# Where GpSimd's operand sums stand among its other work, in a retention and feed-forward kernel on one core

## The chip, the core and the metric

The kernel runs on one NeuronCore of a Trainium2 chip. TensorE (PE in the profile) does the matmuls, with weight loads shown apart as PEld; VectorE (DVE), ScalarE (ACT) and GpSimd (POOL) do the elementwise work; SyncE (SP) issues nearly all DMAs, in program order on one queue. The metric is device time in microseconds (us) for the whole program, one launch.

## The reference

A retention layer (attention without softmax, with a fixed decay) feeds a two-layer feed-forward network with the activation h·cos(h):

```python
B, H, S, D_ = q.shape                       # 8, 8, 576, 64
scores = scale * np.matmul(q, k.transpose(0, 1, 3, 2))
gamma = 1.0 - 2.0 ** (-5.0 - np.arange(H))
Dmat = np.where(rel >= 0, gamma[:, None, None] ** rel[None, :, :], 0.0)   # rel = i - j
x = np.matmul(scores * Dmat, v)             # then reshaped to 4608 tokens x 512
h = x @ w_in                                # 512 -> 2048
g = h * np.cos(h)
out = g @ w_out                             # 2048 -> 512, float32
```

## The kernel before, in words

**Groups.** The 4608 tokens are 36 groups of 128. `load(g)` issues the DMAs for q, k and v of one group on SP's queue. `prep(g)` runs on GpSimd (lines 137, 138 and 144; line 146 once in nine groups): it scales q and k by their share of the decay, casts v, and leaves bf16 tiles `qks` and `vb`. `transposes(g)` (line 153) is from group 6 on a DMA on SP's queue that turns `qks` into `qkT`; for groups 4 and 5 TensorE does it. Retention is then matmuls per group: `scores` (line 180, masked by VectorE into `ret`, line 189), `states` (line 239, summed by VectorE, lines 260 and 262) and `attn_out` (lines 280 and 293, evacuated into `xT`, line 305).

**Tiles.** The feed-forward part walks ten tiles of tokens, n = 0 to 9, of widths 512, 256, 256 and then seven times 512. For a tile, `mm1` (line 320) computes h for 1024 columns at a time into PSUM; ScalarE takes the cosine (line 328) and VectorE multiplies (line 329) into `gT`, of which there is one buffer. Tiles 0 to 2 multiply with `w_out` plainly (`mm2`, line 337). Tiles 3 to 9 (from `S7 = 3` on) use `mm2_seven`: the product of a 2x2 block split is made from seven block products (line 430) in the order 3, 4, 5, 2, 1, 7, 6, instead of eight. Products 3 and 4 need differences of quarters of `w_out` (`w_sums(3)` and `w_sums(4)`, written in place into `w_out_sb`); products 1, 6 and 7 need three more sums of quarters (`ws`); products 5, 2, 1, 7 and 6 need sums of quarters of `gT` (`gs`, made by `g_sum`, line 395). `gs5` is made on VectorE, the others on GpSimd, except `gs1` of tile 3. From tile 4 on they are made in two halves, after the fourth and the eighth `mm1` block; in tile 3 the first part of `gs5` and `gs2` is emitted after the seventh block and all the rest after the eighth. Each product is 16 matmuls.

**What sets the order.** The scheduler is in manual mode: each engine runs its instructions in the order in which the program emits them. The retention work of coming groups is put between the products of a tile by hand, through `at` (`scores2` and `unit7`, ahead of the product named). `feed(s)` is called each time a block of 128 output tokens is stored (s = 0 to 35, four per wide tile), just after the store's DMA was emitted, and it emits the next `prep`, `transposes` and `load` calls. So on GpSimd the sums of a tile stand ahead of the preparation that `feed` emits during that tile's products, and on SP's queue stores, transposing DMAs and loads stand in the order of the calls. The tile pools hold 5 loaded groups (`ld`), 8 prepared (`nat`) and 8 transposed ones (`trp`); an instruction that writes a buffer waits for the last reader of what it held.

The rule by which `feed` decides, before (late tiles prepare only what had been loaded by an earlier call):

```python
while prepared < min(before if s >= late_from else loaded, NG, 2 * s + 7, s + 11):
    prep(prepared)
```

The functions that the diff touches, with the line numbers of the profile:

Of the kernel before, what the change touches and what calls it, by code (L numbers as in the profile page):

```python
# [13 lines left out]
ALU = mybir.AluOpType  # L14
# [3 lines left out]
def kernel(  # L18
# [16 lines left out]
    nc = tc.nc  # L35
# [18 lines left out]
    assert sum(widths) == NTOK  # L54
    starts = [sum(widths[:n]) for n in range(len(widths))]
    N_PE_T = 6

    consts = ctx.enter_context(tc.tile_pool(name="consts", bufs=1))
    first = ctx.enter_context(tc.tile_pool(name="first", bufs=1))
    ld = ctx.enter_context(tc.tile_pool(name="ld", bufs=5))  # L60
    nat = ctx.enter_context(tc.tile_pool(name="nat", bufs=8))
    trp = ctx.enter_context(tc.tile_pool(name="trp", bufs=8))
    retp = ctx.enter_context(tc.tile_pool(name="retp", bufs=4))
# [86 lines left out]
    def transposes(g, banks=None, only=(0, 1)):  # L150
        qks, vb, qkT, qT = tiles["a", g]
        if g >= N_PE_T:
            nc.sync.dma_start(qkT, qks.rearrange("s m h d -> s (m h d)"), transpose=True)  # L153
            return
        for m in only:
            ps = psum.tile([P, HG, P], BF16, tag=banks[m], name="tr")
            for hg in range(HG):
                nc.tensor.transpose(
                    ps[:, hg, :],
                    qks[:, m, 2 * hg : 2 * hg + 2, :].rearrange("s h d -> s (h d)"),  # L160
                    ident,
                )
            nc.scalar.copy(qkT[:, m * HG : (m + 1) * HG, :], ps)
        if ("fv", g) in tiles and g != 3:
            nc.scalar.copy(vb, tiles.pop(("fv", g)))
# [193 lines left out]
    def w_sums(x, e0, e1):  # L359

        a, b, op_ = {
            3: ((0, 1), (1, 1), ALU.subtract),
            4: ((1, 0), (0, 0), ALU.subtract),
            1: ((0, 0), (1, 1), ALU.add),
            6: ((0, 0), (0, 1), ALU.add),
            7: ((1, 0), (1, 1), ALU.add),
        }[x]
        if x in (3, 4):
            w_sum[x] = w_quarter(*a)
        elif x not in w_sum:  # L370
            pool, tag = {1: (consts, "ws1"), 6: (first, "qs4"), 7: (first, "qT4")}[x]
            w_sum[x] = pool.tile([P, E2, N2], BF16, tag=tag, name=f"ws{x}")
        nc.vector.tensor_tensor(
            out=w_sum[x][:, e0:e1],
            in0=w_quarter(*a)[:, e0:e1],
            in1=w_quarter(*b)[:, e0:e1],
            op=op_,
        )

    def g_sum(n, x, e0, e1):  # L380

        gT = tiles["g", n]
        a, b, op_ = {
            5: ((0, 0), (0, 1), ALU.add),
            2: ((1, 0), (1, 1), ALU.add),
            1: ((0, 0), (1, 1), ALU.add),
            7: ((0, 1), (1, 1), ALU.subtract),
            6: ((1, 0), (0, 0), ALU.subtract),
        }[x]
        if ("gs", n, x) not in tiles:  # L390
            tiles["gs", n, x] = sump.tile([P, E2, 256], BF16, tag=f"gs{x}", name=f"gs{x}")
        i0, i1 = (
            gT[:, k * E2 + e0 : k * E2 + e1, r * 256 : (r + 1) * 256] for r, k in (a, b)
        )
        (nc.vector if x == 5 or (n, x) == (S7, 1) else nc.gpsimd).tensor_tensor(  # L395
            out=tiles["gs", n, x][:, e0:e1], in0=i0, in1=i1, op=op_
        )

    def sums_after(n, i):

        if n == S7:
            if i < 4:
                w_sums(3 + i % 2, i // 2 * 4, i // 2 * 4 + 4)
            if i == 6:
                g_sum(n, 5, 0, 4)
                g_sum(n, 2, 0, 4)
            elif i == 7:
                for x, e in ((5, 4), (2, 4), (1, 0), (7, 0), (6, 0)):
                    g_sum(n, x, e, E2)
        elif i in (3, 7):  # L410
            for x in (5, 2, 1, 7, 6):
                g_sum(n, x, i - 3, i + 1)
# [26 lines left out]
    def mm2_seven(n, at):  # L439

        s0 = starts[n] // P

        def new(tag):
            return op.tile([P, 2, N2], F32, tag=tag, name="ot")

        def store(t, r, c, s):
            r0 = starts[n] + r * 256
            nc.sync.dma_start(
                out[r0 : r0 + 256, c * N2 : (c + 1) * N2].rearrange("(j p) c -> p j c", p=P), t
            )  # L450
            feed(s)

        for x in (3, 4, 5, 2, 1, 7, 6):
            for u in at.get(x, []):
                u()
            product(n, x)
            if x == 3:
                u22 = new("a")
                nc.scalar.copy(u22, tiles["o", 3])
            elif x == 4:  # L460
                nc.vector.tensor_tensor(out=u22, in0=tiles["o", 4], in1=u22, op=ALU.add)
            elif x == 5:
                c12, u11 = new("c"), new("b")
                nc.scalar.copy(c12, tiles["o", 3])
                nc.vector.tensor_tensor(out=u11, in0=u22, in1=tiles["o", 3], op=ALU.subtract)
                store(c12, 0, 1, s0)
            elif x == 2:
                c21 = new("d")
                nc.scalar.copy(c21, tiles["o", 4])
                nc.vector.tensor_tensor(out=u22, in0=u22, in1=tiles["o", 4], op=ALU.subtract)  # L470
                store(c21, 1, 0, s0 + 1)
            elif x == 1:
                nc.vector.tensor_tensor(out=u11, in0=tiles["o", 1], in1=u11, op=ALU.add)
            elif x == 7:
                nc.vector.tensor_tensor(out=u11, in0=tiles["o", 7], in1=u11, op=ALU.add)
                store(u11, 0, 0, s0 + 2)
            elif x == 6:
                nc.vector.tensor_tensor(out=u22, in0=tiles["o", 1], in1=u22, op=ALU.add)
                store(u22, 1, 1, s0 + 3)
# [3 lines left out]
    def feed(s):  # L483

        nonlocal loaded, prepared, transposed
        before = loaded
        late_from = starts[S7] // P
        while True:
            while prepared < min(before if s >= late_from else loaded, NG, 2 * s + 7, s + 11):
                prep(prepared)  # L490
                prepared += 1
                if transposed < N_PE_T:
                    transposed += 1

            if N_PE_T <= transposed < min(prepared, s + 11) and (
                transposed <= loaded - 2 or loaded == NG or (s > 3 and loaded == before)
            ):
                transposes(transposed)
                transposed += 1
            elif loaded < min(NG, 2 * s + 8, s + 13):  # L500
                load(loaded)
                loaded += 1
            else:
                break
# [131 lines left out]
        if not soon:  # L636
            copy()

    def unit7(g, more=True):

        copy = states([g + 1, g + 2], "b")()
        attn_out([g, g + 1], "m", nc.scalar.copy)
        if more:
            scores2(g + 2)
        copy(nc.scalar.copy)

    late = []
    for n, w in enumerate(widths):
# [14 lines left out]
        for i, (et, c0, cw) in enumerate(blocks):  # L663

            inside = {
                (0, 0): {2: lambda: (attn_out([3], "n"), state(3))},
                (1, 0): {4: lambda: scores(5, "a")},
                (1, 1): {3: lambda: attn_out([5], "a", evac=nc.scalar.copy)},
            }.get((n, i), {})
            mm1(n, et, c0, cw, banks[i], inside)  # L670
            if (n, i) == (3, 1):
                late.pop()()
            if n == 2 and i < 3:
                for e in (0, 4):
                    w_sums((1, 6, 7)[i], e, e + 4)
            if n >= S7:
                sums_after(n, i)

        g = starts[n] // P + w // P
        if n == 0:  # L680
            todo = [
                (45, lambda: transposes(4, "ab")),
                (49, lambda: state(4)),
                (50, lambda: scores(4, "a")),
                (57, lambda: attn_out([4], "a")),
                (61, lambda: transposes(5, "ba")),
                (63, lambda: state(5)),
            ]
        elif n == 1:
            todo = pair(6, "ab", 16, 27)  # L690
        elif n == 2:
            todo = [(11, lambda: scores2(g)), (25, lambda: unit(g, "m", soon=True))]
            late += [lambda: unit(g + 2, "b", False)]
        else:
            at = {}
            if n + 1 < len(widths):
                at = {5: [lambda: unit7(g)], 1: [lambda: unit7(g + 2, n > S7)]}
                if n in (3, 4):
                    at[4] = [lambda: scores2(g)]
            mm2_seven(n, at)  # L700
            continue
        todo.sort(key=lambda u: u[0])
# [42 lines left out]
```

## Time and profile before

| what | value |
|---|---|
| time, median of 6 runs | 324.21 us (323.46 to 325.91) |
| the profiled execution's own time | 323.46 us |
| its span on the core | 321.8 us, mean granted TensorE clock 0.991 |
| TensorE busy | 293.7 us (91%) |
| GpSimd busy | 218.5 us (68%) |
| VectorE busy | 210.1 us (65%) |
| ScalarE busy | 139.3 us (43%) |
| sums on GpSimd (line 395) | 52 instructions, 116.0 us |

All positions in the text are us from the start of the profiled span. The profiled execution spends 1.7 us outside the span (323.46 less 321.8). A busy share is a mean over stages with different limits, so the views used below are those with positions: the timelines of single engines, which give start, duration, engine, line, operation, tiles and, in square brackets, how long the engine had been idle just before and what ended that; the list of waits (total us, times, longest); and the chain of work that ended last.

### The profile page before, as it was taken

The numbers are of one execution on the slowest core, as the hardware profiler recorded it, in microseconds if no ns is written. First come the engines' busy times: TensorE is split into PE (matmuls) and PEld (weight loads), VectorE is DVE, ScalarE is ACT, GpSimd is POOL, SyncE is SP. The second block draws the span as 40 slices with busy tenths as digits, with TensorE's granted clock in tenths as the row PEclk, the third lists the DMA queues.
The fourth block names the chain that finished last, engine by engine and source line by source line (L and its number), as shares of the span: only waits on it lengthen the run. The fifth ranks groups of instructions, "written<-read, shape, count | busy, mean of one in ns | idle before, by whom it ended". The sixth has DMA issues, their size and how long they took to land.

```text
span 321.8 us, 6585 instructions
## 1 busy us (share of the span) xinstructions
PE 293.7 (91%) x2724; PEld 199.5 (62%) x2745; DVE 210.1 (65%) x242; ACT 139.3 (43%) x176; POOL 218.5 (68%) x179
## 2 busy tenths in 40 slices
PE   8899999996998697997999899989998899899984
PEld 3478458573487585456745674567557754784573
DVE  5776335659499972687658765776478548935762
ACT  3656225232155252642356334633464346425610
POOL 2760165455544799599967996799769946950893
PEclk9999999999799999999999999999999999999998
DMA  8999999999999994999199909990999060021012
GB/s 210 210 212 207 196 226 207 172 203 251 155 237 182 233 205 93 232 215 171 37 223 212 208 3 194 245 212 7 181 242 209 26 163 2 0 67 65 2 55 76
DMA packets 154109, 50.23 MB, mean 156 GB/s; under 512 B 140768, under 2 KB 153056, under 8 KB 154080
## 3 DMA queue, kind: packets, MB, share of 16 engines
q1 hardware_dynamic: 149856, 45.63, 73.7%
q0 software_dynamic: 4224, 4.19, 7.9%
q8 instruction: 21, 0.34, 0.4%
q14 instruction: 8, 0.07, 0.1%
HBM read 36.70 MB, written 9.44 MB: 143 GB/s over the span
## 4 chain that ended last, share of the span: by engine, by line
PE 38%; POOL 24%; DMA 16%; SPq 11%; DVE 4%; issue 4%; ACT 2%; POOLq 1%
PE h L320 20%; POOL gs L395 17%; PE o L430 8%; DMA fq<-in_q_dram 7%; SPq L112 7%; DMA fk<-in_k_dram 6%; PE o L337 6%; SPq L153 3%; POOL qks L138 3%; DMA fv<-in_v_dram 2%; POOL qks L137 2%; ACT cosh L328 2%; DVE gT L329 2%; POOL vb L144 2%; PE sc L180 1%
## 5 line engine op out<-in xcount | busy, mean ns | idle before, releaser
L395 POOL TENSOR_TENSOR gs<-gT 128x1024 bf16<-128x1024 bf16 (+1 forms) x52 | 116.0, 2266 | 20.4 <-DVE gT L329 20.4
L320 PE MATMUL h<-xT,w_in_sb 128*128 128x512 bf16 (+2 forms) x820 | 127.2, 313 | 1.7 <-DVE gT L329 0.9
L329 DVE TENSOR_TENSOR gT<-h,cosh 128x1024 bf16<-128x1024 f32 x72 | 87.9, 1222 | 42.6 <-ACT cosh L328 42.6
L328 ACT ACTIVATE cosh<-h,half_pi 128x1024 f32<-128x1024 f32 x72 | 80.2, 1113 | 81.0 <-PE h L320 77.6
L320 PEld LDWEIGHTS <-w_in_sb 128*128 128x128 bf16 x832 | 76.0, 98 | 50.1 <-issue 1.7
L137 POOL TENSOR_TENSOR qks<-fq,gq 128x512 bf16<-128x512 f32 x32 | 34.7, 1084 | 60.0 <-DMA fq<-in_q_dram 57.9
L430 PEld LDWEIGHTS <-gs 128*128 128x128 bf16 x560 | 53.0, 98 | 17.1 <-POOL gs L395 9.0
L138 POOL TENSOR_TENSOR qks<-fk,gk 128x512 bf16<-128x512 f32 x35 | 36.9, 1054 | 13.6 <-DMA fk<-in_k_dram 13.0
L189 DVE TENSOR_TENSOR ret<-sc,tri 128x1024 bf16<-128x1024 f32 x32 | 37.9, 1216 | 4.8 <-PE sc L180 4.7
L430 PE MATMUL o<-ws,gs 128*128 128x256 bf16 x336 | 38.6, 273 | 2.1 <-POOL gs L395 2.1
L337 PE MATMUL o<-w_out_sb,gT 128*128 128x512 bf16 x121 | 30.3, 393 | 2.7 <-DVE gT L329 2.3
L430 PE MATMUL o<-w_out_sb,gs 128*128 128x256 bf16 x224 | 26.5, 273 | 5.3 <-POOL gs L395 4.6
L305 ACT CAST xT<-ov 128x1024 bf16<-128x1024 f32 (+1 forms) x18 | 16.5, 917 | 31.3 <-PE ov L293 31.2
L430 PE MATMUL o<-w_out_sb,gT 128*128 128x256 bf16 x224 | 25.9, 273 | 0.0
L430 PEld LDWEIGHTS <-gT 128*128 128x128 bf16 x224 | 21.7, 98 | 4.0
L144 POOL CAST vb<-fv 128x512 bf16<-128x512 f32 x32 | 20.9, 652 | 3.1 <-DMA fv<-in_v_dram 2.6
L337 PEld LDWEIGHTS <-gT 128*128 128x128 bf16 x128 | 12.1, 100 | 16.4 <-issue 2.7
L395 DVE TENSOR_TENSOR gs<-gT 128x1024 bf16<-128x1024 bf16 (+1 forms) x15 | 17.4, 1168 | 0.4
L180 PE MATMUL sc<-qkT 64*128 64x128 bf16 x256 | 12.2, 220 | 5.9 <-DVE s L262 3.7
L253 ACT CAST sb<-s 64x256 bf16<-64x256 f32 x40 | 16.1, 403 | 0.6
L180 PEld LDWEIGHTS <-qkT 64*128 64x128 bf16 x288 | 8.6, 95 | 12.3 <-issue 8.2
L347 ACT COPY ot<-o 128x512 f32<-128x512 f32 x8 | 4.7, 588 | 22.1 <-PE o L337 22.1
(72 smaller groups left out, 181.7 us busy)
## 6 DMA issues: line engine op xcount, KB each, us to landing
out_dram<-ot SPq DMA_DIRECT2D x36, 256.0 KB, 3.9
fk<-in_k_dram SPq DMA_DIRECT2D x32, 256.0 KB, 5.0
fv<-in_v_dram SPq DMA_DIRECT2D x32, 256.0 KB, 5.1
fq<-in_q_dram SPq DMA_DIRECT2D x28, 256.0 KB, 4.1
w_in_sb<-in_moe_w_in_dram POOLq DMA_DIRECT2D x4, 512.0 KB, 9.0
w_out_sb<-in_moe_w_out_dram POOLq DMA_DIRECT2D x4, 512.0 KB, 16.2
fq<-in_q_dram SPq DMA_DIRECT2D x2, 512.0 KB, 4.4
fq<-in_q_dram SPq DMA_DIRECT2D x8, 128.0 KB, 4.4
```

The costliest lines, as they stand in the source:

```text
L112: i = nc.sync.dma_start(f[p0:p1], src[b, :, s0 : s0 + p1 - p0, :].rearrange("h s d -> s h d"))
L137: nc.gpsimd.tensor_tensor(out=qks[:, 0], in0=fq, in1=tq, op=ALU.mult)
L138: (nc.vector if g == 3 else nc.gpsimd).tensor_tensor(out=qks[:, 1], in0=fk, in1=tk, op=ALU.mult)
L144: nc.gpsimd.tensor_copy(vb, fv)
L180: nc.tensor.matmul(ps[:, he, hg, :], lhsT=qkT[d0 : d0 + D, HG + hg, :], rhs=qT[d0 : d0 + D, hg, :], start=True, stop=True,)
L189: nc.vector.tensor_tensor(out=ret.rearrange("p a b i -> p (a b) i"), in0=ps.rearrange("p a b i -> p (a b) i"), in1=mask.unsqueeze(1).to_br ...
L320: nc.tensor.matmul(ps[:, j, :], lhsT=w_in_sb[:, dg, (et + j) * P : (et + j + 1) * P], rhs=xT[:, dg, c0 : c0 + w], start=(dg == 0), stop=(d ...
L328: nc.scalar.activation(cosh, ps, ACTF.Sin, bias=half_pi, scale=1.0)
L329: nc.vector.tensor_mul(gT[:, et : et + m, c0 : c0 + w], ps, cosh)
L337: nc.tensor.matmul(ps, lhsT=gT[:, et, tsi * P : (tsi + 1) * P], rhs=w_out_sb[:, et, :], start=(et == 0), stop=(et == ET - 1),)
L395: (nc.vector if x == 5 or (n, x) == (S7, 1) else nc.gpsimd).tensor_tensor(out=tiles["gs", n, x][:, e0:e1], in0=i0, in1=i1, op=op_)
L430: nc.tensor.matmul(ps[:, j], lhsT=lhs[:, e, j * P : (j + 1) * P], rhs=rhs[:, e, :], start=(x in (3, 4, 1, 7) and e == j == 0), stop=(e == ...
```

## The change

Six edits, all in the order or the place of work; what is computed stays the same.

1. `w_sums(3)` and `w_sums(4)` run on GpSimd, each as one instruction over 128x2048, emitted after the first `mm1` block of tile 3. Before, they were four VectorE instructions over 128x1024 after the first four blocks.
2. `w_sums` for 1, 6 and 7 (six VectorE instructions) move from tile 2's `mm1` into the `mm2` of tile 0.
3. In each half of a tile's `g_sum` calls the first sum on GpSimd gets a dependency on VectorE's `gs5` of the same half.
4. In tiles 3 and 4 the two `unit7` calls move from ahead of products 5 and 1 to ahead of products 2 and 7; in the others VectorE's addition `both` is emitted after the `states` additions of the first unit, not before them.
5. From s = 8 on (tile 3 and later) `feed` prepares to a count per store, 0, 1, 1 and 2 groups, and the transposing DMAs follow at once.
6. From s = 8 on `feed` then loads until five groups are loaded ahead of those prepared. For s below 8 its rule is as before.

Built, the program has on SP's queue the same order of DMAs as before up to the first store of tile 3, and on GpSimd the same order but for the two `w_out_sb` sums, which stand behind the preparation of group 17 and ahead of tile 3's `gs`.

```diff
@@ -54,10 +54,11 @@
     assert sum(widths) == NTOK
     starts = [sum(widths[:n]) for n in range(len(widths))]
     N_PE_T = 6
+    LD = 5
 
     consts = ctx.enter_context(tc.tile_pool(name="consts", bufs=1))
     first = ctx.enter_context(tc.tile_pool(name="first", bufs=1))
-    ld = ctx.enter_context(tc.tile_pool(name="ld", bufs=5))
+    ld = ctx.enter_context(tc.tile_pool(name="ld", bufs=LD))
     nat = ctx.enter_context(tc.tile_pool(name="nat", bufs=8))
     trp = ctx.enter_context(tc.tile_pool(name="trp", bufs=8))
     retp = ctx.enter_context(tc.tile_pool(name="retp", bufs=4))
@@ -370,7 +371,7 @@
         elif x not in w_sum:
             pool, tag = {1: (consts, "ws1"), 6: (first, "qs4"), 7: (first, "qT4")}[x]
             w_sum[x] = pool.tile([P, E2, N2], BF16, tag=tag, name=f"ws{x}")
-        nc.vector.tensor_tensor(
+        (nc.gpsimd if x in (3, 4) else nc.vector).tensor_tensor(
             out=w_sum[x][:, e0:e1],
             in0=w_quarter(*a)[:, e0:e1],
             in1=w_quarter(*b)[:, e0:e1],
@@ -392,15 +393,25 @@
         i0, i1 = (
             gT[:, k * E2 + e0 : k * E2 + e1, r * 256 : (r + 1) * 256] for r, k in (a, b)
         )
-        (nc.vector if x == 5 or (n, x) == (S7, 1) else nc.gpsimd).tensor_tensor(
+        i = (nc.vector if x == 5 or (n, x) == (S7, 1) else nc.gpsimd).tensor_tensor(
             out=tiles["gs", n, x][:, e0:e1], in0=i0, in1=i1, op=op_
         )
+        if x == 5:
+            tiles["gate"] = i
+        elif "gate" in tiles:
+            tc.add_manual_dep(
+                i.ins,
+                tiles.pop("gate").ins.name,
+                mybir.DependencyInfo(mybir.DependencyClass.Sync, mybir.DependencyReason.DATA),
+                reason="port free",
+            )
 
     def sums_after(n, i):
 
         if n == S7:
-            if i < 4:
-                w_sums(3 + i % 2, i // 2 * 4, i // 2 * 4 + 4)
+            if i == 0:
+                w_sums(3, 0, E2)
+                w_sums(4, 0, E2)
             if i == 6:
                 g_sum(n, 5, 0, 4)
                 g_sum(n, 2, 0, 4)
@@ -450,15 +461,18 @@
             )
             feed(s)
 
+        def both():
+            nc.vector.tensor_tensor(out=u22, in0=tiles["o", 4], in1=u22, op=ALU.add)
+
         for x in (3, 4, 5, 2, 1, 7, 6):
-            for u in at.get(x, []):
-                u()
+            if x in at:
+                at[x](*[both] * (x == 5))
+            elif x == 5:
+                both()
             product(n, x)
             if x == 3:
                 u22 = new("a")
                 nc.scalar.copy(u22, tiles["o", 3])
-            elif x == 4:
-                nc.vector.tensor_tensor(out=u22, in0=tiles["o", 4], in1=u22, op=ALU.add)
             elif x == 5:
                 c12, u11 = new("c"), new("b")
                 nc.scalar.copy(c12, tiles["o", 3])
@@ -484,9 +498,20 @@
 
         nonlocal loaded, prepared, transposed
         before = loaded
-        late_from = starts[S7] // P
+        n, r = divmod(s - starts[S7] // P, 4)
+        if n >= 0:
+            while prepared < min(NG, starts[S7] // P + 10 + 4 * n + (0, 1, 2, 4)[r]):
+                prep(prepared)
+                prepared += 1
+            while transposed < prepared:
+                transposes(transposed)
+                transposed += 1
+            while loaded < min(NG, prepared + LD):
+                load(loaded)
+                loaded += 1
+            return
         while True:
-            while prepared < min(before if s >= late_from else loaded, NG, 2 * s + 7, s + 11):
+            while prepared < min(loaded, NG, 2 * s + 7, s + 11):
                 prep(prepared)
                 prepared += 1
                 if transposed < N_PE_T:
@@ -636,9 +661,10 @@
         if not soon:
             copy()
 
-    def unit7(g, more=True):
+    def unit7(g, more=True, then=lambda: None):
 
         copy = states([g + 1, g + 2], "b")()
+        then()
         attn_out([g, g + 1], "m", nc.scalar.copy)
         if more:
             scores2(g + 2)
@@ -670,15 +696,15 @@
             mm1(n, et, c0, cw, banks[i], inside)
             if (n, i) == (3, 1):
                 late.pop()()
-            if n == 2 and i < 3:
-                for e in (0, 4):
-                    w_sums((1, 6, 7)[i], e, e + 4)
             if n >= S7:
                 sums_after(n, i)
 
         g = starts[n] // P + w // P
         if n == 0:
             todo = [
+                (34 + 5 * i, lambda x=x, e=e: w_sums(x, e, e + 4))
+                for i, (x, e) in enumerate((x, e) for x in (1, 6, 7) for e in (0, 4))
+            ] + [
                 (45, lambda: transposes(4, "ab")),
                 (49, lambda: state(4)),
                 (50, lambda: scores(4, "a")),
@@ -694,9 +720,16 @@
         else:
             at = {}
             if n + 1 < len(widths):
-                at = {5: [lambda: unit7(g)], 1: [lambda: unit7(g + 2, n > S7)]}
+                at = {
+                    5: lambda then: unit7(g, True, then),
+                    1: lambda: unit7(g + 2),
+                }
                 if n in (3, 4):
-                    at[4] = [lambda: scores2(g)]
+                    at = {
+                        4: lambda: scores2(g),
+                        2: lambda: unit7(g),
+                        7: lambda: unit7(g + 2, n > 3),
+                    }
             mm2_seven(n, at)
             continue
         todo.sort(key=lambda u: u[0])
```

## The prediction

> **What bounds the kernel now.** First the page's busy times, and the shares of the chain that ended last:
>
> ```profile
> PE 293.7 (91%) x2724; PEld 199.5 (62%) x2745; DVE 210.1 (65%) x242; ACT 139.3 (43%) x176; POOL 218.5 (68%) x179
> ...
> PE 38%; POOL 24%; DMA 16%; SPq 11%; DVE 4%; issue 4%; ACT 2%; POOLq 1%
> ```
>
> TensorE is nearly full, yet the chain passes through it for 38% only, and through GpSimd, loads and SP's queue for 51%. So what can be won is TensorE's idle time, and GpSimd's position decides much of it. TensorE's timeline gives the gaps in brackets:
>
> ```profile
> 112.70 0.32 PE L239 MATMUL st<-v_odd,qks 128*64 128x64 bf16 x8 [2.13 <-DVE ret L189]
> ...
> 125.02 1.92 PE L430 MATMUL o<-ws,gs 128*128 128x256 bf16 x16 [1.62 <-POOL gs L395]
> ...
> 184.59 1.05 PE L430 MATMUL o<-w_out_sb,gs 128*128 128x256 bf16 x8 [1.54 <-POOL gs L395]
> ...
> 316.83 1.05 PE L430 MATMUL o<-ws,gs 128*128 128x256 bf16 x8 [0.16 <-POOL gs L395]
> ```
>
> Further gaps, not shown: 1.73 us at 147.2 and 0.68 at 155.1 in tile 4, 1.23 at 279.4 in tile 8. Tiles 5, 6 and 7 each lose 1.5 us (1.54, 1.48, 1.55) at product 2, whose second half of `gs2` is late. GpSimd's timeline says why, and what happens ahead of tile 3:
>
> ```profile
> 109.22 1.98 POOL L137 TENSOR_TENSOR qks<-fq,gq 128x512 bf16<-128x512 f32 x1 [0.61 <-DMA fq<-in_q_dram]
> ...
> 170.90 1.04 POOL L137 TENSOR_TENSOR qks<-fq,gq 128x512 bf16<-128x512 f32 x1 [3.51 <-DMA fq<-in_q_dram]
> ...
> 173.63 17.15 POOL L395 TENSOR_TENSOR gs<-gT 128x1024 bf16<-128x1024 bf16 x8
> ```
>
> In tile 5 the sums could start at 170.85, when VectorE's first `gs5` ends; they start at 173.63 behind a preparation that waited 3.51 us for its load. Group 17, prepared at 109.22 to 112.74, is the last ahead of tile 3's sums. The chain in order of time shows what paces it:
>
> ```profile
> 93.17 5.99 DMA fk<-in_k_dram
> ...
> 103.50 5.58 DMA fq<-in_q_dram
> ```
>
> Each of these loads is followed there by a preparation (99.22, 109.22), the first also by the transposing DMA behind which SP issues the next load (101.29). It is a ring of load, preparation, transposing DMA and next load, with TensorE in none of its links.
>
> **The two `w_out` sums on GpSimd: the loss.** For s below 8 the order on SP and GpSimd is unchanged, so group 17 is ready as before, less what VectorE's sums cost it: the 1.98 us scaling takes 1.04 where nothing collides, and VectorE's tile 3 sums will now lie near 102, not at 108 to 110. So 112.74 - 0.94 = 111.8. Only then does GpSimd do `w_sums(3)` and `w_sums(4)`. Their price is a row of the same shape:
>
> ```profile
> L395 POOL TENSOR_TENSOR gs<-gT 128x2048 bf16<-128x2048 bf16 x2 | 8.1, 4065 | 0.0
> ...
> L395 DVE TENSOR_TENSOR gs<-gT 128x2048 bf16<-128x2048 bf16 x1 | 1.2, 1210 | 0.0
> ```
>
> Start to start such sums lie 4.02 us apart (116.88 to 120.90), so `ws3` is ready at 115.8 and `ws4` at 119.9. Product 3, first after tile 3's `mm1`, reads `ws3`: it ran at 105.49 before, and would be ready near 101 (below), so TensorE idles some 14 us. From 119.9 on follow products 4, 5, 2, 1, 7 and 6 at 1.84 us (105.49 to 107.33 for 16 matmuls), one unit with scores (1.94, 112.70 to 114.64) and one without (1.49, 118.24 to 119.73): 11.04 + 3.43 = 14.5, end at 134.4. GpSimd's own end, 119.9 + 12.25 = 132.1 (its four sums took 12.25 us from 112.71), is ready before product 6 needs it. Tile 3 ended at 126.8 before: a loss of 7.6 us.
>
> To this comes the clock after so long an idle time. The windows over tile 2:
>
> ```profile
> 75.00:80.00 5.00, 2.66 (x18) 0.97 (x17) 5.00 (x6) 0.83 (x1) 2.84 (x4) 1.00 1.23 258
> 80.00:85.00 5.00, 4.24 (x19) 1.77 (x19) 2.97 (x3) 0.58 (x1) 2.40 (x4) 0.66 1.13 189
> ```
>
> After 2.34 us idle out of 5 the granted clock was 0.66 over the next 5, that is 0.34 x 5 = 1.7 us of work lost. Here product 3 and `scores2` (1.84 + 0.6) have 4.1 us before `ws4` comes, so 1.6 us of such a loss are covered: it costs 0.1 with the row's 1.7, and 1.8 if twice as much is lost. I take 0.8, in the middle, since the row shows one restart only. Loss: 7.6 + 0.8 = 8.4 us. [...]
>
> [...] The rows above say 4.07 against 1.21, 3.4 times. [...]
>
> **What tiles 2 and 3 gain is swallowed.** The sums moved out of tile 2 free VectorE there: TensorE's gaps of 0.43, 1.87 and 1.18 us and the 1.7 us at low clock go, and in tile 3 0.74 us at 99.9. All of it makes TensorE arrive at product 3 earlier, near 101, and wait longer; likewise the 2.13 and 1.62 us of tile 3 are replaced by the sum above. In tile 0 the moved sums cost nothing while VectorE's idle 9 us (35.2 to 44.2) hide them; without that cover, 6 x 0.7 us.
>
> **The gains, tiles 4 to 8.** Tile 4: product 5 now lies between `scores2` and the unit's `states`, and 1.84 us cover the 1.73; the second unit comes after product 1, whose VectorE addition waits for no ScalarE copy, and its 0.68 us go: 2.41. Tiles 5 to 7: loads are issued a tile ahead, so four preparations run without pause, 4 x 2.55 = 10.2 us (124.92 to 127.47 for one), after the sums' 17.15. That is 27.4 of a 31.3 us tile; GpSimd is free when `gs5` ends, some 2.7 us sooner than before, against 1.5 needed. Gain 1.54 + 1.48 + 1.55, and 2 x 0.16 us that TensorE lost in the first units' scores. What is next late is the 0.57 to 0.69 us at the second unit's scores, which stay. Tile 8: VectorE's second `gs5` took 2.56 us, against 0.69 for the first at 268.37:
>
> ```profile
> 275.27 2.56 DVE L395 TENSOR_TENSOR gs<-gT 128x1024 bf16<-128x1024 bf16 x1
> ```
>
> It came 0.1 us after GpSimd's fourth sum had begun and waited for it. With the new dependency GpSimd starts some 0.6 us later, so its third ends just after 275.27, and VectorE gets in after 0.1 to 0.4 us: the 1.23 us go, and the `states` additions ahead of `both` help. Sum: 2.41 + 4.89 + 1.23 = 8.5 us. Bounds: 6 if the dependency misses the slot (up to 2.0 us in VectorE, of which TensorE's products cover most), 9.5 if the second units' gaps shrink too.
>
> **The last tile.** Its end hangs on GpSimd's last sum (the 0.16 gap above). The wait for `gs5` (299.77) moves the start: 299.77 + 0.1 + 17.15 = 317.0, against 316.77: a loss of 0.25 us. What is queued behind that wait on GpSimd is the rest of the tile's sums, which TensorE needs only there so closely. On SP's queue, transposing DMAs and loads now come behind the second store of each tile; group 18's data are ready near 136 and needed past 150, so this costs nothing, and up to 2 us if the first loads of tile 3, held until its first store near 125, arrive late.
>
> **The sum.** 8.4 + 0.25 - 8.5 = +0.2: 323.7 us against the profiled 323.46. The median lies 0.75 above that execution, so 324.4.
>
> **Rivals.** *Slower:* the moved sums collide with GpSimd's preparations of groups 4 to 6 (38.6 to 50.6), at the head of the ring; each collision can cost what the 1.98 us row shows, 0.94, so up to 6 x 0.94 = 5.6, of which loads awaited (1.1 and 1.2 us ahead of group 6) absorb part. At half, 327.2; it decides from 1.4 us on, since ready times from there to group 17 shift one for one. Against it: VectorE can do four of the six before GpSimd starts at 38.56. *Faster:* the same collisions vanish at 71 to 108 (rows 0.36, 0.23, 0.46, 0.42 and 0.23 us too long, 1.7 in all), and if the ring takes all of it and loads come 2 us quicker, 320.7. Against it: most of those preparations had waited for loads, so the ring gains little. *It does not do what it says:* product 3 isn't held, as if the sums stood ahead of the preparations; then tiles 2 and 3 keep their gains too (5.2 + 4.5), about 306. The built order speaks against it.
>
> **Chances.** 0.5% (1.6 us) is about what a measurement of this kernel can tell from no change. Forecast, within that: 0.43. Slower rival, or the clock and late loads at their upper bounds (up to 328.5): 0.32. Faster: 0.25, of which 0.03 the last rival. The forecast's own range is 322.6 to 325.8; 319.5 to 328.5 leaves out about 2 in 10.
>
> **What would show it.** Right: TensorE idle from about 101 to 116, ended by GpSimd's line 374; granted clock near half after it; tile 3 ending near 135; no wait for `gs` at product 2 of tiles 5 to 7; second `gs5` below 1.1 us; no load wait ahead of GpSimd's late preparations. Wrong: product 3 starting before 112 or after 119, or late tiles no shorter than 32.5 us.

## The result and the profile after

The changed kernel took 322.43 us (median of 24 runs) against 324.26 for the kernel before (50 runs): a ratio of 0.9933, 95% interval 0.9916 to 0.995. The ratio leaves out slow executions on both sides, one of them of 1671.57 us. In the study's first batch the same two programs gave 321.12 against 322.45, ratio 0.9965 (0.9936 to 0.9994). So the change is faster by about 0.5%, where the forecast had no change. The forecast time, 324.4, is 2.0 us too high: the result lies 0.2 us below the forecast's own range (322.6 to 325.8) and inside the wider one (319.5 to 328.5).

The first profiled execution of the changed kernel started disturbed (a granted TensorE clock of 0.5, called half clock below, from 20.2 to 27.1 us), so the profile shown here is of a second one, own time 321.17, span 319.5. It stands beside a second execution of before on the same chip, own time 322.43, span 320.7. Page, busy times, and the chain that ended last:

```profile
PE 291.4 (91%) x2724; PEld 200.1 (63%) x2745; DVE 199.1 (62%) x238; ACT 139.4 (44%) x176; POOL 223.4 (70%) x181
...
PE 69%; SPq 8%; DMA 8%; POOL 7%; DVE 2%; issue 2%; ACT 1%; POOLq 1%
```

TensorE carries 69% of the chain where it carried 38%, GpSimd 7% where it carried 24%. One would expect a gain far above 0.5% from that. TensorE's timeline shows where it went (start, duration, engine, line, operation, tiles; in brackets the idle time before and what ended it):

```profile
94.84 4.09 PE L321 MATMUL h<-xT,w_in_sb 128*128 128x256 bf16 x36
114.18 3.57 PE L441 MATMUL o<-w_out_sb,gT 128*128 128x256 bf16 x16 [15.25 <-POOL w_out_sb L374]
117.68 0.68 PE L181 MATMUL sc<-qkT 64*128 64x128 bf16 x16
118.29 1.92 PE L441 MATMUL o<-w_out_sb,gT 128*128 128x256 bf16 x16
...
149.60 0.40 PE L181 MATMUL sc<-qkT 64*128 64x128 bf16 x8 [0.38 <-DVE gT L330]
190.23 0.40 PE L181 MATMUL sc<-qkT 64*128 64x128 bf16 x8 [0.57 <-DVE s L263]
221.08 0.40 PE L181 MATMUL sc<-qkT 64*128 64x128 bf16 x8 [0.68 <-DVE s L263]
252.06 0.40 PE L181 MATMUL sc<-qkT 64*128 64x128 bf16 x8 [0.57 <-DVE s L263]
```

The last four rows are all of TensorE's waits in tiles 4 to 8: the 1.5 us ahead of product 2, the 1.73 and the 1.23 are gone. Against that stands one wait of 15.25 us in tile 3, ended by line 374 on GpSimd, and product 3 behind it takes 3.57 us where the row of the same shape at 118.29 takes 1.92. GpSimd's timeline over the same place:

```profile
109.51 0.61 POOL L145 CAST vb<-fv 128x512 bf16<-128x512 f32 x1
110.08 8.05 POOL L374 TENSOR_TENSOR w_out_sb<-w_out_sb 128x2048 bf16<-128x2048 bf16 x2
118.09 12.27 POOL L396 TENSOR_TENSOR gs<-gT 128x1024 bf16<-128x1024 bf16 x4
```

Group 17 is ready at 110.12, then the two sums take 8.0 us, then the operand sums 12.3. TensorE's next tile starts at 133.2.

The two executions by their terms, in us (a tile is counted from its first `mm1` matmul to the next tile's):

| term | before | after | difference | forecast |
|---|---|---|---|---|
| group 17 ready | 111.45 | 110.12 | -1.33 | -0.94 |
| from there to the end of tile 3 | 14.03 | 23.05 | +9.0 | +9.3 |
| end of tile 3 | 125.5 | 133.2 | +7.7 | +8.4 |
| tile 4 | 33.84 | 31.67 | -2.17 | -2.41 |
| tiles 5 to 7 | 98.49 | 92.81 | -5.68 | -4.89 |
| tile 8 | 30.72 | 29.31 | -1.41 | -1.23 |
| last tile | 28.32 | 28.63 | +0.31 | +0.25 |
| last matmul ends | 316.85 | 315.59 | -1.26 | about +0.2 |

### The profile page after: what moved, and what is told of

Read it like the earlier page. It is cut to its first block, busy times and chain, and to the rows that moved or that the text cites. A ratio compares the mean times of both kernels' runs of the same rounds, so it can differ in the third digit from the quotient of the medians.

```text
span 324.0 us, 6597 instructions
## 1 busy us (share of the span) xinstructions
PE 294.9 (91%) x2724; PEld 201.9 (62%) x2745; DVE 204.0 (63%) x238; ACT 139.3 (43%) x176; POOL 223.9 (69%) x181
## 4 chain that ended last, share of the span: by engine, by line
PE 59%; DMA 12%; SPq 11%; POOL 9%; issue 3%; DVE 3%; ACT 1%; POOLq 1%
PE h L321 28%; PE o L441 21%; SPq L113 8%; DMA fv<-in_v_dram 6%; POOL gs L396 5%; DMA fk<-in_k_dram 5%; PE o L338 4%; SPq L154 3%; PE sc L181 2%; PE ov L294 1%; POOL w_out_sb L374 1%; DMA fq<-in_q_dram 1%; POOL qks L139 1%; PE ov L281 1%; DMA out_dram<-ot 1%
## 5 line engine op out<-in xcount | busy, mean ns | idle before, releaser
L321 PE MATMUL h<-xT,w_in_sb 128*128 128x512 bf16 (+2 forms) x820 | 128.9, 316 | 3.0 <-DMA w_in_sb<-in_moe_w_in_dram 1.7
L321 PEld LDWEIGHTS <-w_in_sb 128*128 128x128 bf16 x832 | 76.9, 99 | 52.1 <-DMA w_in_sb<-in_moe_w_in_dram 1.9
L139 POOL TENSOR_TENSOR qks<-fk,gk 128x512 bf16<-128x512 f32 x35 | 38.0, 1084 | 11.3 <-DMA fk<-in_k_dram 10.8
L441 PE MATMUL o<-w_out_sb,gT 128*128 128x256 bf16 x224 | 27.6, 283 | 13.1 <-POOL w_out_sb L374 13.1
L338 PE MATMUL o<-w_out_sb,gT 128*128 128x512 bf16 x121 | 28.8, 380 | 0.4 <-issue 0.2
L145 POOL CAST vb<-fv 128x512 bf16<-128x512 f32 x32 | 19.5, 611 | 3.8 <-DMA fv<-in_v_dram 3.2
L294 PE MATMUL ov<-ret,vb 128*64 128x128 bf16 x288 | 12.3, 225 | 1.4 <-DVE vb L631 1.4
L396 DVE TENSOR_TENSOR gs<-gT 128x1024 bf16<-128x1024 bf16 (+1 forms) x15 | 12.2, 822 | 0.4
```

The costliest lines, as they stand in the source:

```text
L139: (nc.vector if g == 3 else nc.gpsimd).tensor_tensor(out=qks[:, 1], in0=fk, in1=tk, op=ALU.mult)
L145: nc.gpsimd.tensor_copy(vb, fv)
L321: nc.tensor.matmul(ps[:, j, :], lhsT=w_in_sb[:, dg, (et + j) * P : (et + j + 1) * P], rhs=xT[:, dg, c0 : c0 + w], start=(dg == 0), stop=(d ...
L338: nc.tensor.matmul(ps, lhsT=gT[:, et, tsi * P : (tsi + 1) * P], rhs=w_out_sb[:, et, :], start=(et == 0), stop=(et == ET - 1),)
L396: i = (nc.vector if x == 5 or (n, x) == (S7, 1) else nc.gpsimd).tensor_tensor(out=tiles["gs", n, x][:, e0:e1], in0=i0, in1=i1, op=op_)
L441: nc.tensor.matmul(ps[:, j], lhsT=lhs[:, e, j * P : (j + 1) * P], rhs=rhs[:, e, :], start=(x in (3, 4, 1, 7) and e == j == 0), stop=(e == ...
```

## Experiments

### The changed kernel again

No edit.

> The changed kernel once more, to see the ready time of group 17 in another execution. Theory 1 (the wait sets tile 3): TensorE waits for GpSimd's line 374 again, tile 3 ends 23.3 us after group 17 is prepared, as in the first profile (114.4 to 137.7), and since the median is 1.8 us below the kernel before, group 17 must be ready near 110.5 in an ordinary execution, so tile 3 ends near 134. Rival (gain elsewhere): group 17 is ready at 112.7 or later as before, and the 2 us come from tiles 4 to 9, which then take less than 181 us.

It gave the profile and the ratio above (0.9965). Group 17 was ready at 110.12 and tile 3 ended 23.05 us behind it, near what the theory said (110.5 and 23.3); tiles 4 to 9 took 182.4 us, where the rival said less than 181.

### The kernel before again

No edit.

> The kernel before once more, for a second profile: is group 17 ready at 112.7 again? Theory 1 as sized in the prediction has the ready time fixed by loads to within 1 us. Rival: it moves by 2 us and more between executions of the same kernel.

322.43 us (one run). The end of group 17's preparation on GpSimd, and the start of tile 4 on TensorE:

```profile
110.85 0.60 POOL L144 CAST vb<-fv 128x512 bf16<-128x512 f32 x1
111.42 12.24 POOL L395 TENSOR_TENSOR gs<-gT 128x1024 bf16<-128x1024 bf16 x4
```

```profile
125.48 2.75 PE L320 MATMUL h<-xT,w_in_sb 128*128 128x512 bf16 x11
```

Group 17 was ready at 111.45, 1.3 us earlier than in the execution that the forecast was made from (112.74), between the two expectations, and tile 3 ended 1.3 us earlier too. The distance from one to the other is 14.03 us in both. So between these two executions of one program the ring's position moved by more than a microsecond, and what follows it did not.

### The two `w_out` sums back on VectorE

```diff
-        (nc.gpsimd if x in (3, 4) else nc.vector).tensor_tensor(
+        nc.vector.tensor_tensor(
...
-            if i == 0:
-                w_sums(3, 0, E2)
-                w_sums(4, 0, E2)
+            if i < 4:
+                w_sums(3 + i % 2, i // 2 * 4, i // 2 * 4 + 4)
```

> The changed kernel with the two in-place w_out sums back on VectorE, in four pieces, at their place of before; all else as changed. Theory 1: the 13 us wait at product 3 goes, tile 3 then ends with GpSimd's own sums, some 14 us after group 17 is ready instead of 23.3, so about 9 us less: near 313 us, a ratio to the kernel before of 0.966. Rival: the wait only hides a wait that comes next (the later groups' loads and preparations, which start from the same time), and the time stays near 322.

312.58 us, ratio to before 0.9689 (0.9666 to 0.9713). Tile 3 ends at 124.6, 14.0 us behind group 17 (110.59), as before the change. The late tiles have the changed kernel's lengths to 0.1 us. What TensorE now waits for in tile 3 is `gs2`, by its timeline:

```profile
103.92 1.91 PE L440 MATMUL o<-w_out_sb,gs 128*128 128x256 bf16 x16
...
112.73 1.89 PE L440 MATMUL o<-w_out_sb,gs 128*128 128x256 bf16 x8 [4.22 <-POOL gs L396]
```

### The two `w_out` sums on GpSimd, alone

The reverse of the diff above, on the kernel before.

> The kernel before with one edit alone: the two in-place w_out sums on GpSimd, at the place of the changed kernel. Theory 1: tile 3 ends 23 us after group 17 is ready (112.7 before), near 136 instead of 126.8, and the late tiles keep their length: 332 to 333 us. Rival (the wait is absorbed by later slack, since late tiles wait for loads that now have more time): 324 to 328 us.

331.63 us, ratio 1.0287 (1.0247 to 1.0327). Tile 3 ends 22.9 us behind group 17 (135.5 against 112.63), and tile 4 on keeps the length of before (192.2 us from there to the last matmul, against 191.4). TensorE's timeline has the same waiting place, shorter because TensorE comes to it later with the other sums still in tile 2:

```profile
116.69 3.57 PE L431 MATMUL o<-w_out_sb,gT 128*128 128x256 bf16 x16 [10.07 <-POOL w_out_sb L373]
```

The two halves multiply to the whole: 1.0287 x 0.9689 = 0.9967, and the change itself measured 0.9965 in the batch of the first experiment. Edit 1 costs about 9 us and the other five edits bring about 10.

### The six early sums back in tile 2

```diff
+            if n == 2 and i < 3:
+                for e in (0, 4):
+                    w_sums((1, 6, 7)[i], e, e + 4)
...
-                (34 + 5 * i, lambda x=x, e=e: w_sums(x, e, e + 4))
-                for i, (x, e) in enumerate((x, e) for x in (1, 6, 7) for e in (0, 4))
```

> The changed kernel with the w_out sums for products 1, 6 and 7 back in tile 2, as before. The prediction held that moving them was worth nothing, because TensorE's wait at product 3 swallows what tile 2 gains. Theory 1a (swallowed): group 17 ready at 110 to 110.6 as in the changed kernel, time unchanged near 321.1. Theory 1b (the moved sums let the ring of loads and preparations run sooner, which is the 2 us that the prediction missed): group 17 ready at 111.5 to 112.7 as in the three profiles with the sums in tile 2, tile 3's end as much later, 322.6 to 323.7 us.

322.88 against 322.75 for before: ratio 0.9997 (0.9974 to 1.002). Tile 2 grew from 16.25 to 20.65 us, but tile 3 ended only 1.5 us later (134.7 against 133.2). So two thirds of the 4.4 us vanish into the wait, which is 11.84 us here. The ready time lies between those of the two theories, the time in that of theory 1b. What came through has two parts: group 17 is ready at 110.85 instead of 110.12 (0.7), and the other 0.8 lies behind the restart. The windows of this kernel (busy time and count of PE, PEld, DVE, ACT and POOL, then granted clock, DMA share, GB/s):

```profile
114.00:118.00 4.00, 3.10 (x15) 2.16 (x15) 0.00 (x0) 0.00 (x0) 4.00 (x2) 0.50 1.23 269
118.00:121.00 3.00, 3.00 (x30) 2.08 (x28) 1.94 (x2) 0.59 (x1) 3.00 (x3) 0.62 0.60 99
```

and of the changed kernel:

```profile
114.00:118.00 4.00, 3.82 (x26) 2.55 (x27) 0.00 (x0) 0.21 (x1) 4.00 (x2) 0.52 1.24 263
118.00:121.00 3.00, 3.00 (x39) 2.63 (x34) 2.82 (x3) 0.38 (x1) 3.00 (x3) 1.00 0.44 72
```

In the changed kernel full clock is back at 117.8, before `ws4` lets product 4 start; here half clock lasts until 120.3, through the scores and half of product 4 (1.04 and 2.34 us, 0.68 and 1.92 there). That this edit caused the 0.8 is not shown: in the changed kernel and the next three versions below, all with the early sums in tile 0, the distance from group 17 to the end of tile 3 was 23.05, 22.92, 23.58 and 23.31 us; full clock was back 3.7 us after the restart in the first and 4.9 in the third.

### The old rule for preparations and loads

`feed` has the rule of before for all s (the whole block for tile 3 on is removed). This undoes edits 5 and 6 together; they were not taken apart.

> The changed kernel with the feeding rule of before (one group prepared per store, loads no further ahead). Theory (loads ahead are what frees GpSimd for the sums): preparations wait for loads again, the sums of tiles 5 to 7 start late and product 2 waits 1.5 us in each: some 4.6 us more, near 325.7, ratio to the kernel before 1.010. Rival (the gain of tiles 4 to 8 comes from the order of TensorE's work and the dependency): 321 to 322 us.

328.35 us, ratio 1.0176 (1.0149 to 1.0202): 2.6 us above the expectation and slower than the kernel before. Tiles 4 to 7 grew by 0.57, 2.77, 2.22 and 1.73 us. TensorE's wait at product 2 of tile 5, and GpSimd's timeline ahead of it:

```profile
190.06 1.05 PE L441 MATMUL o<-w_out_sb,gs 128*128 128x256 bf16 x8 [2.14 <-POOL gs L396]
```

```profile
176.36 1.04 POOL L138 TENSOR_TENSOR qks<-fq,gq 128x512 bf16<-128x512 f32 x1 [3.74 <-DMA fq<-in_q_dram]
177.48 1.04 POOL L139 TENSOR_TENSOR qks<-fk,gk 128x512 bf16<-128x512 f32 x1
178.54 0.61 POOL L145 CAST vb<-fv 128x512 bf16<-128x512 f32 x1
179.11 17.15 POOL L396 TENSOR_TENSOR gs<-gT 128x1024 bf16<-128x1024 bf16 x8
```

A preparation waits 3.74 us for its load and holds the sums behind it, as in the profile of before, and by more: the wait at product 2 is 2.14 us here where it was 1.54. Why the old rule costs more here than in the kernel before is not traced. In the changed kernel the sums start when `gs5` lets them:

```profile
171.15 0.61 POOL L145 CAST vb<-fv 128x512 bf16<-128x512 f32 x1
175.19 17.18 POOL L396 TENSOR_TENSOR gs<-gT 128x1024 bf16<-128x1024 bf16 x8 [3.43 <-DVE gs L396]
```

GpSimd is ready 3.4 us before it is let go. The forecast had named this link and put the lateness at 2.7 us; in the run without loads ahead it is 3.7 (`gs5` ended at 175.42, the sums began at 179.11).

### No dependency of GpSimd's sums on `gs5`

```diff
-        if x == 5:
-            tiles["gate"] = i
-        elif "gate" in tiles:
-            tc.add_manual_dep(i.ins, tiles.pop("gate").ins.name, ...)
```

> The changed kernel without the dependency of GpSimd's first sum on VectorE's gs5. Theory (GpSimd then starts with VectorE, its fourth sum begins 0.1 us before VectorE's second gs5 comes, as in tile 8 before): that gs5 takes 2.56 us instead of 0.8 in tiles 4 to 8, and TensorE's scores in the first units wait 0.7 us in four tiles and product 5 0.45 in tile 4; the last tile ends 0.3 us sooner: 2.9 us more, near 324.0, ratio 1.005. Rival (VectorE has slack, the dependency is idle): 320.8, 0.3 us less than the changed kernel.

325.06 us, ratio 1.0062 (1.0036 to 1.0087), 1.1 us above the expectation. Tiles 4 to 8 are longer by 0.84, 0.82, 0.39, 0.82 and 0.82 us, the last tile shorter by 0.31. The other 0.5 us lies in tile 3, where half clock lasted until 119.0 (117.8 in the changed kernel); that the edit caused this is not shown. VectorE's timeline in tile 5, without the dependency:

```profile
175.68 0.69 DVE L396 TENSOR_TENSOR gs<-gT 128x1024 bf16<-128x1024 bf16 x1
182.59 2.57 DVE L396 TENSOR_TENSOR gs<-gT 128x1024 bf16<-128x1024 bf16 x1
```

and in the changed kernel:

```profile
174.35 0.69 DVE L396 TENSOR_TENSOR gs<-gT 128x1024 bf16<-128x1024 bf16 x1
181.26 0.78 DVE L396 TENSOR_TENSOR gs<-gT 128x1024 bf16<-128x1024 bf16 x1
```

Without the dependency a GpSimd sum had begun at 182.49, 0.1 us before VectorE's second `gs5` was due; with it the next GpSimd sum begins at 181.44, 0.2 us after `gs5`. So the dependency moves GpSimd's chain of sums, and `gs5` comes just before the start of one of them instead of just after it. It costs 0.3 us once, in the last tile, and saves 0.4 to 0.8 in each of five.

### The two units ahead of products 5 and 1 again, in tiles 3 and 4

```diff
-                    at = {4: ..., 2: lambda: unit7(g), 7: lambda: unit7(g + 2, n > 3)}
+                    at[4] = lambda: scores2(g)
+                    at[1] = lambda: unit7(g + 2, n > 3)
```

> The changed kernel with the place of the two units in tiles 3 and 4 undone: they stand ahead of products 5 and 1 again. Theory (the gain of tile 4 was this edit's 2.41 by the forecast, less what loads ahead bring there): the waits of 1.73 and 0.68 us at the units' states and scores come back in tile 4, which is 33.4 to 34.1 us long instead of 31.67; tile 3 still ends where GpSimd's second w_out sum lets it, about 133; time about 323. Rival (tile 4's gain came from loads issued ahead and the order of VectorE's addition): tile 4 stays below 32.3, time 321 to 322.

323.02 us, ratio 1.0011 (0.9985 to 1.0038). Tile 4 took 33.09 us, between the two expectations. The two waits are back, the first smaller than in before:

```profile
153.03 0.32 PE L240 MATMUL st<-vb,qks 128*64 128x64 bf16 x8 [0.94 <-DVE ret L190]
...
160.90 0.40 PE L181 MATMUL sc<-qkT 64*128 64x128 bf16 x8 [0.68 <-DVE s L263]
```

So 1.4 of tile 4's 2.2 us belong to the units' place. The rest goes with loads and the dependency, whose removal cost this tile 0.57 and 0.84; these parts overlap and do not add.

### All of tile 3's sums on VectorE

On top of the version with the `w_out` sums on VectorE (its wait of 4.22 us is shown above):

```diff
-        i = (nc.vector if x == 5 or (n, x) == (S7, 1) else nc.gpsimd).tensor_tensor(
+        i = (nc.vector if x == 5 or n == S7 else nc.gpsimd).tensor_tensor(
```

> The changed kernel with the two w_out sums on VectorE (as in e2) and, in tile 3 alone, all sums of gT on VectorE as well. Theory 1: tile 3 then waits for nothing on GpSimd; it ends when TensorE's own work ends, about 119 instead of 124.6, so 5.5 us below e2: 307 us, ratio 0.952. Rival (the groups needed in tile 3 and 4 are themselves late, since the ring prepares group 17 no sooner than 110): 310 to 312 us.

311.97 us, ratio 0.9659 (0.9631 to 0.9686): the expected 5 us did not come, tile 3 ends at 124.2. VectorE's timeline, and TensorE's:

```profile
101.97 6.50 DVE L396 TENSOR_TENSOR gs<-gT 128x1024 bf16<-128x1024 bf16 x5
108.40 1.21 DVE L190 TENSOR_TENSOR ret<-sc,tri 128x1024 bf16<-128x1024 f32 x1
109.54 1.21 DVE L190 TENSOR_TENSOR ret<-sc,tri_mix 128x1024 bf16<-128x1024 f32 x1
```

```profile
110.89 0.43 PE L240 MATMUL st<-v_odd,qks 128*64 128x64 bf16 x8 [4.79 <-DVE ret L190]
...
114.18 3.31 PE L440 MATMUL o<-w_out_sb,gs 128*128 128x256 bf16 x16
117.33 1.91 PE L440 MATMUL o<-ws,gs 128*128 128x256 bf16 x16
```

The wait of 4.22 us for GpSimd's `gs2` became one of 4.79 us for VectorE's `ret`, which stood behind 6.5 us of sums. It is the fault of the change again, on the other engine. The time is the rival's, but not by its cause, late groups.

The wait costs more than itself. Behind it the unit's matmuls and the scores took 3.29 us (110.89 to 114.18) where the kernel before took 1.94 (112.70 to 114.64), and product 2 (114.18) took 3.31 us where product 1 behind it took 1.91: by these rows an estimated 2.8 us lost. The execution's mean granted clock, 0.989 over 310.4 us, amounts to an estimated 6.8 us at half clock (2 x 0.011 x 310.4). The same stands behind the 4.22 us of the version before: 1.89 us for eight matmuls at 112.73, where eight at 184.59 in the kernel before took 1.05.

### Sums behind the first pair's `ret`

On top of the version just shown:

```diff
-        i = (nc.vector if x == 5 or n == S7 else nc.gpsimd).tensor_tensor(
+        i = (nc.vector if x == 5 or (n == S7 and x != 6) else nc.gpsimd).tensor_tensor(
...
-                for x, e in ((5, 4), (2, 4), (1, 0), (7, 0), (6, 0)):
+                for x, e in ((5, 4), (2, 4), (6, 0)):
...
-                        4: lambda: scores2(g),
+                        4: lambda: (scores2(g), n == S7 and [g_sum(n, x, 0, E2) for x in (1, 7)]),
```

> Edit on the kernel with w_out sums 3 and 4 back on VectorE: in tile 3 gs2, gs1 and gs7 also on VectorE, gs1 and gs7 emitted behind scores2's ret; only gs6 stays on GpSimd. That kernel's TensorE waited 4.22 us for GpSimd's gs2 (ended by group 17's preparation at 110.59) and tile 3 ended at 124.6, time 312.58. In the version with all sums on VectorE the wait was 4.79 us for ret, which stood behind 6.50 us of sums on VectorE. Theory (the wait moves to whatever stands last in an engine's queue, and here nothing does): product 2 starts at about 108.5, then products 2 and 1, the unit, 7 and 6: 4 x 1.84 + 1.49 = 8.9, tile 3 ends at 117.5 to 118.5, time 306. Rival (the moved sums collide with the preparations of groups 16 and 17 and with ret of the second pair, so both engines lose what TensorE gains): tile 3 ends at 122 or later, 310 to 312.

309.51 us, ratio 0.9594 (0.9569 to 0.9618): faster than both kernels, and than all other versions, if not the 306 expected. Its profiled execution (314.53) began tile 3 late; a second profile of the same version follows.

> The version with gs1 and gs7 behind the first pair's ret once more, for a profile without the late start of tile 2 (18.71 us long there, 16.25 in the others). Its timed runs gave 309.5, 3.1 below the version with three sums on GpSimd, whose tile 3 ended at 124.6. Theory: tile 3 ends at about 121.5 and the wait for VectorE's state addition at the second scores, 3.50 us in the first look, is above 2 us. Rival (that wait belonged to the late start alone): it is below 1 us and tile 3 ends below 120.

308.84 us (one run). Tile 3 ends at 120.8, and the wait for VectorE's state addition is 2.63 us, about as the theory said:

```profile
110.48 0.61 PE L181 MATMUL sc<-qkT 64*128 64x128 bf16 x8 [2.63 <-DVE s L263]
111.03 3.11 PE L440 MATMUL o<-w_out_sb,gs 128*128 128x256 bf16 x16
```

In front of that addition VectorE had `gs1` and `gs7`, 2.57 us. Product 2 behind the wait again ran slowly: it took 3.11 us, and product 1 behind it, at 113.97, took 1.91. The mean granted clock, 0.994 over 307.1 us, amounts to an estimated 3.7 us at half clock.

### Sums behind the whole first unit

`gs1` and `gs7` emitted after `unit7(g)` at product 2 instead.

> The version before this one (gs2, gs1 and gs7 of tile 3 on VectorE, gs1 and gs7 behind the first pair's ret) with gs1 and gs7 moved once more, behind the whole first unit. There the second unit's scores waited 3.50 us for VectorE's state addition, which stood behind gs1 and gs7 (3.19 us). Theory (a wait stands wherever a sum stands ahead of retention work in an engine's queue): with the sums behind the unit that wait is below 0.6 us, product 2 starts at about 109, and tile 3 ends at 118 to 119; the time falls from 309.5 to 306 to 307. Rival (the sums then hold product 1 instead, and GpSimd's gs6 holds product 6 behind group 17's preparation): tile 3 ends at 121 or later, 309 or more.

312.95 us (312.53 to 313.72), ratio 0.9697 (0.9669 to 0.9726). The wait for the state addition fell to 0.38 us, but `gs1` then held product 1, as the rival said:

```profile
114.44 1.92 PE L440 MATMUL o<-w_out_sb,gs 128*128 128x256 bf16 x16
118.09 1.92 PE L440 MATMUL o<-ws,gs 128*128 128x256 bf16 x16 [1.73 <-DVE gs L396]
```

From the start of product 3 to the end of tile 3 this version took 20.9 us (104.06 to 124.94), the one before it 21.8 (98.96 to 120.81): 1 us less. That is not less waiting: TensorE waited 3.7 us there in four waits, 3.6 in two in the version before. But behind none of the four did the matmuls slow down: product 2 took 1.92 us instead of 3.11. The time is worse because tile 2 took 19.1 us instead of 16.25, behind a transposing DMA that TensorE awaited for 2.08 us, and tile 3's `mm1` took 2 us longer, its first 32 matmuls 4.70 us instead of 3.66. Nothing in the edit touches tile 2, and in the first profiled execution of the version before it took 18.71 us. Why all four runs of this version came out near 313 is not settled.

## Why the prediction was wrong

The mechanism was right in the main, link by link. The step that failed is the sum 8.4 + 0.25 - 8.5: both large terms were mis-sized, and in directions that add. The loss in tile 3 measured 7.7 us instead of 8.4; the gains behind it, with the last tile's loss taken off, measured 8.95 instead of 8.25. Their difference, which the forecast called "no change", is a gain of 1.3 us in the profiles and of 0.4 to 0.7% in the medians. Both terms were worked out from a single execution. None of the forecast's signs of being wrong appeared: product 3 started at 114.18 and tiles 4 to 8 took 29.3 to 31.7 us.

**The loss in tile 3: right place, 0.7 us too large.** Of the forecast's signs of being right, TensorE was idle from 98.9 to 114.2 (said: about 101 to 116), ended by line 374, and the clock stood at 0.5 after it. Half of the error lies ahead of the sums: "112.74 - 0.94" took off one collision's worth; between the two executions of the same chip it is 1.33, and the base itself was a late execution. With the early sums back in tile 2 the group was ready at 110.85; the other versions that keep them in tile 0 and shared the changed kernel's order up to there had it at 110.06 to 110.59. So 0.3 to 0.8 us of the 1.33 goes with the sums taken out of tile 2, and the rest is no more than two executions of one kernel differ by. The other half lies behind: the distance of tile 3's end from group 17 was 23.05 us (said: 23.4). It came that near in part by luck, since two of its terms were off and partly cancel, as follows.

**The clock: the term of 0.8 was nearly all covered.** The forecast took the middle between 0.1 and 1.8 us. In the changed kernel full clock returned at 117.8, 3.7 us after the restart, while `ws4` came only at 118.13: product 4 began 0.16 us after `ws4`, so the clock cost no more than that. The runs had half-clock stretches of 3.4, 6.8, 13.7 and 17.0 us (last section). How much is paid differs from execution to execution: at most 0.16 us here, 0.8 more in the run with the early sums undone. Against this, product 4 and what follows it took 14.9 us where the forecast had 14.5; in it the second pair of scores waited 0.56 us for VectorE's state addition, a wait like those of tiles 5 to 7, which the forecast had left out here.

**"What tiles 2 and 3 gain is swallowed": two thirds.** Undoing that edit cost 4.4 us in tile 2 and 1.5 at the end of tile 3, of which 0.7 is the group's ready time and 0.8 the clock behind the restart; that the edit caused the 0.8 is not shown.

**The gains of tiles 4 to 8: right, 0.7 us too small.** Tile 4 gave 0.2 less, tiles 5 to 7 0.8 more (5.68 instead of 4.89), tile 8 0.2 more. Half of the 0.8 is one wait of 0.38 us, at tile 5's first scores, which the execution used for the forecast did not show and the second one did; the rest is not traced. The dependency's bound of "6 if the dependency misses the slot" did not come: it met the slot in each of tiles 4 to 8, where VectorE's second `gs5` took 0.78 to 0.81 us. In tile 5 that sum took 2.57 us without the dependency and 0.78 with it; the first, of the same size, took 0.69 in both.

**The rivals.** *Slower* did not come as such: the preparations of groups 4 and 6 did collide with the moved sums (VectorE's at 37.29 to 39.19, 46.35 and 47.83: group 4's first scaling took 1.59 us at 38.50, group 6's two took 1.48 and 1.51 us at 46.45 and 47.90; 1.04 each before), but group 6's last cast ended at 50.1, between the 49.8 and 50.6 of the two executions of before, which had waited there for loads too. *Faster* (collisions gone, the ring sooner) is the direction in which it went: 2.0 us below the forecast's median where the rival had 3.7. But of the 1.5 us by which the profiles differ from the forecast, only 0.4 is the ring. *Product 3 not held* is, in effect, the version with the `w_out` sums on VectorE; the forecast gave 306 for it and it measured 312.6, since `gs2`, still behind group 17 on GpSimd, then holds product 2 for 4.22 us, and the eight matmuls behind the wait took 1.89 us instead of 1.05.

## What to carry to other kernels

When two large terms cancel, forecast their difference with the terms' own errors, and take positions from more than one execution: here one program's ring moved 1.3 us between two executions, as much as the whole net effect. Before moving work to a slower, idler engine, list what stands ahead of it in that engine's queue and who waits for it: four sums on VectorE, 3.9 us together (0.67 to 1.53 each), became a step of 8 us on GpSimd, behind a preparation whose data they did not need. And profile again after each repair: four versions of tile 3 turned one wait into the next (15.25 for a sum, 4.22 for `gs2`, 4.79 for `ret`, 2.63 for a state addition) and the least of them is the best kernel, 4% faster than before. Behind each of these waits the matmuls also ran slower: 3.57 us for 16 instead of 1.92, 1.89 for eight instead of 1.05, 3.31 and 3.11 for 16 instead of 1.91. In the last two versions four short waits (3.7 us together) cost 1 us less than two, the longer of 2.63 (3.6 together).

## What the runs showed of the hardware

The half-clock stretches of which the profiles give both ends were 3.4 us long (kernel before, 80.7 to 84.1), 6.8 and 13.7 (first profile of the changed kernel, 20.2 to 27.1 and 109.0 to 122.7), 13.6 (its second, 104.2 to 117.8) and 17.0 (without the dependency, 102.0 to 119.0): near multiples of 3.4. After the long wait in tile 3 half clock lasted 3.7 us past the restart in the changed kernel, 4.9 without the dependency and 5.4 with the early sums back in tile 2; in the changed kernel 16 matmuls took 3.57 us in it instead of 1.92. The length of a wait alone did not tell whether the matmuls behind it ran slower: in the second execution of before, after a wait of 2.94 us (ended at 112.41), 32 matmuls at 114.35 took 3.67 us, as 32 did at full clock in the first (114.64), while in the version with the sums behind the whole unit, after one of 2.08 us (ended at 83.90), 32 matmuls at 86.38 took 4.70 us where the version before had 3.66.

A VectorE sum of 0.69 us stretched to 2.57 when it was due 0.1 us after a GpSimd sum of 2.12 us had begun (tile 5 without the dependency; in tile 8 of the kernel before 2.56, at 275.27 behind 275.17). GpSimd paid as well: of its eight sums of that tile 8 the two that began while VectorE made a `gs5`, at 268.48 and 277.25, took 2.57 us each, the others 2.12 to 2.13. Its eight sums of tile 5 took 17.68 us without the dependency and 17.18 with it; in the first profile of the changed kernel, where they took 17.17, one of them took 2.57 (185.98, with VectorE's `gs5` at 185.80).
